# A decayed linear attention and a mixture of experts on one core: the next unit's scores issued behind the state update, and the accumulator banks divided anew

## The chip, the core and the metric

The kernel runs on one core of a Trainium2 chip. The metric is the device time of one execution in microseconds (us). The engines of the core work in parallel, each through its own queue in order: TensorE (PE in the profile, its weight loads as PEld), VectorE (DVE), ScalarE (ACT), GpSimd (POOL) and the queue SP, which issues DMAs. TensorE writes into the accumulator memory PSUM, here divided into eight banks of 512 float32 values for each of 128 partitions. VectorE and ScalarE read it from there.

## The reference

```python
batch, n_heads, seq, head_dim = (4, 8, 768, 48)          # r, k, v, w: (4, 8, 768, 48); u: (8, 48)
for t in range(S):
    cur = einsum('bhd,bhe->bhde', u * k[t], v[t])
    y[t] = einsum('bhd,bhde->bhe', r[t], state + cur)
    state = w[t][..., None] * state + einsum('bhd,bhe->bhde', k[t], v[t])
x = y.transpose(0, 2, 1, 3).reshape(3072, 384)           # tokens x (heads * head_dim)
p = domain_probs / (domain_probs.sum(-1, keepdims=True) + 1e-9)      # 3072 x 4 experts
for e in range(4):                                       # w1: 4 x 384 x 1024, w2: 4 x 1024 x 384
    out += p[:, e:e+1] * (maximum(x @ w1[e], 0) @ w2[e])
```

All arrays are float32.

## The kernel before

**Units.** The 768 steps are cut into 6 chunks of 128; a chunk of one of the 4 batches is a unit, numbered n = 4 * chunk + batch (0 to 23). A unit has these parts, each with its tile names:
- running products of the decays in both directions (`g` in `after_decays`, `e` in `until_decays`, both scans on VectorE, the second behind two short operations on `zst`), and the multiplication of r and k by them (`scale`, two VectorE operations);
- the scores of k against r, `sc`, 16 TensorE instructions (`scores`), and in the same function k turned round by four transposes into `kt`, which ScalarE copies to `ks`;
- the diagonal from r, k and u (`own_product` on GpSimd, `diag_sum`, `place`), into which `masking` puts the scores under a mask (VectorE) to give `a`;
- the sums `yp`: the state times r, and v times `a` (`values`). ScalarE and VectorE evict them as a high and a low part, and four DMAs (`fill`) put them where the experts read them, as `x`. In chunk 0 there is no state; the sums are then evicted in one copy, as plain float32;
- the new state from `ks` and v (`up`, 16 TensorE instructions), added to the old one (`carry`).

**Steps.** Units 2 to 23 go in five steps: `step_a` (next unit's `after_decays`, this unit's `scores`), `step_b` (next unit's `until_decays`), `step_c` (`masking`), `step_d` (next unit's `scale`, `diag_sum`, `place`) and `step_e` (`values`, `carry`, loads, `fill`, `guard` on ScalarE). The last chunk makes no new state, so its units have neither transposes nor update. Units 2 and 3 have an order of steps of their own; for unit 2 it is a, c, b, d, e. `go()` issues the next step.

**Experts.** A chunk of all four batches (512 tokens) goes through an expert as 8 first products (`f1`: 9 matmuls into one tile `pf1`, read by ScalarE for `hh` (L417) and then by VectorE for `hl` (L418)) and then, for each batch, a second product (`f2`: 24 matmuls into `pf2`). Between them the function `between` gives out steps at a set pace, so that the units' TensorE work lies between the experts' matmuls. Chunk 0 is done first, then chunks 1 and 2 together, then chunks 3, 4 and 5, each group with all experts in turn. From 575 us no unit is left.

**The start.** The first first products use the plain float32 sums of chunk 0, one batch at a time: `begin(b, f)` is `f1` for one batch of 128 tokens, 6 matmuls (L405), of which the start has 8 for batch 0 and 8 for batch 1. Each is a tile of its own in `pf1`, though it fills a quarter of a bank. The order around them is written out by hand (lines 583 to 653 of the file). From tile 3 of batch 0 on it reads

```python
begin(0, 3); until_decays(2); begin(0, 4); begin(0, 5); scale(2); diag_sum(2)
begin(0, 6); split_w2(1); place(2, 0); place(2, 1); begin(0, 7)
begin(1, 0); step_a(2); begin(1, 1); step_c(2); begin(1, 2); split_w2(2); guard(1)
begin(1, 3); step_b(2); begin(1, 4); step_d(2); begin(1, 5); step_e(2)
begin(1, 6); split_w2(3); begin(1, 7); step_a(3)
```

(a shortening of it, without the loads). Batches 2 and 3 follow in tiles of 256 tokens.

**Banks.** `ps_f1` has 3 banks (tiles `pf1`, and the sums of chunk 0), `ps_f2` 2, `ps_sc` one tile of 2 banks, which `sc` and `yp` use in turn, and `ps_mi` 1, which `kt`, `up` and one tile at the end use in turn.

Of the kernel before, what the change touches and what calls it, by code (L numbers as in the profile page):

```python
# [8 lines left out]
F32 = mybir.dt.float32  # L9
# [4 lines left out]
ALU = mybir.AluOpType  # L14
AX = mybir.AxisListType
PS = bass.MemoryType.PSUM

B, H, S, D = 4, 8, 768, 48
NT, DM = B * S, H * D
NE, FF = 4, 1024  # L20
C = 128
NCH = S // C
NP = H // 2
ROWS = 64 + D
KT = DM // 128
# [21 lines left out]
def chunked_path(ctx, tc, dmaj, tmaj, u_bc, probs, w1, w2, out, flag):  # L47
    nc = tc.nc

    def pool(name, bufs, space=None):  # L50
        kw = {} if space is None else {"space": space}
        return ctx.enter_context(tc.tile_pool(name=name, bufs=bufs, **kw))
# [8 lines left out]
    p_wx = pool("wx", 3)  # L61
    p_one = pool("one", 1)
    p_two = pool("two", 2)
    ps_f1 = pool("ps_f1", 3, PS)
    ps_f2 = pool("ps_f2", 2, PS)
    ps_sc = pool("ps_sc", 1, PS)
    ps_mi = pool("ps_mi", 1, PS)


    ident = const.tile([128, 128], F32, name="ident")  # L70
# [6 lines left out]
    st = [const.tile([ROWS, NP, D], F32, name=f"st{b}") for b in range(B)]  # L77
# [4 lines left out]
    sd = [const.tile([ROWS, NP * D + G], F32, name=f"sd{i}") for i in range(2)]  # L82
# [5 lines left out]
    def half(j):  # L88
        return slice(64 * j, 64 * j + D)

    def wide(j):

        return slice(64 * j, 64 if j == 0 else ROWS)
# [67 lines left out]
    un, xb, spare = {}, {}, []  # L161
    NU = B * NCH
# [103 lines left out]
    def scores(n):  # L266

        s = un[n]
        sc = ps_sc.tile([128, 2, NP, C], F32, name="sc", tag="sc")
        for i in range(NP):  # L270
            for j in range(2):
                nc.tensor.matmul(sc[:, j, i, :], s["kk"][half(j), i, :], s["rr"][half(j), i, :],  # L272
                                 start=True, stop=True)
        last = s["c"] == NCH - 1
        if not last:
            kt = ps_mi.tile([128, NP, 128], F32, name="kt", tag="mi")
            for i in range(NP):
                nc.tensor.transpose(kt[:, i, 0:ROWS], s["kk"][:, i, :], ident[0:ROWS, 0:ROWS])  # L278
        s["sc"] = sc
        if not last:  # L280
            ks = p_one.tile([128, NP, ROWS], F32, name="ks", tag="ks")
            nc.scalar.copy(ks, kt[:, :, 0:ROWS])
            s["ks"] = ks
# [6 lines left out]
    def values(n):  # L290
        s = un[n]
        c, b, v = s["c"], s["b"], s["v"]
        if c not in xb:
            xb[c] = p_x.tile([128, KT, B, 2, C], F32R, name="x", tag="x")
        x = xb[c]
        if c == 0:

            y = ps_f1.tile([128, B * C], F32, name="pf1", tag="pf1")[:, 0:KT * C].rearrange("p (i t) -> p i t", i=KT)
            z = vz[n % 2]
            for i in range(KT):  # L300
                for j in range(2):
                    nc.tensor.matmul(y[64 * j:64 * (j + 1), i, :], z[:, j, i, :], s["a"][j][:, KT, :],  # L302
                                     start=(i == 0), stop=False, skip_group_check=True)
                for j in range(2):
                    h = 2 * i + j
                    nc.tensor.matmul(y[half(j), i, :], v[:, h * D:(h + 1) * D], s["a"][j][:, i, :],  # L306
                                     start=False, stop=(i == KT - 1), skip_group_check=True)
            nc.scalar.copy(x_own()[:, :, b], y)
            return


        yp = ps_sc.tile([128, 2, NP, C], F32, name="yp", tag="sc")
        y = [yp[:, i % 2, i // 2, :] for i in range(NP)]
        for i in range(NP):
            for j in range(2):
                o = j ^ (i % 2)
                nc.tensor.matmul(y[i][wide(o)], sd[n % 2][half(j), i * D:i * D + (64 if o == 0 else D)],  # L317
                                 s["rr"][half(j), i, :], start=(i < 2), stop=False, skip_group_check=True)
        for i in range(NP):
            for j in range(2):  # L320
                h = 2 * i + j
                nc.tensor.matmul(y[i][half(j ^ (i % 2))], v[:, h * D:(h + 1) * D], s["a"][j][:, i, :],  # L322
                                 start=False, stop=(i >= 2), skip_group_check=True)
        y3 = s["y3"] = p_two.tile([ROWS, 2, 2, C], F32R, name="y3", tag="y3")

        places = (y3, yp[0:ROWS, 1, 0:2]), (x[0:ROWS, 0::2, b], yp[0:ROWS, 0, 0:2])
        for dst, src in places:
            nc.scalar.copy(dst[:, :, 0], src)  # L328
        for dst, src in places:
            nc.vector.tensor_tensor(dst[:, :, 1], src, dst[:, :, 0].bitcast(F32), ALU.subtract)  # L330

    def last_pair(n):

# [3 lines left out]
    def x_own():  # L337

        if len(spare) < 2:
            spare.append(p_acc.tile([128, B, DM], F32, name="acc", tag="acc").rearrange("p b d -> p (b d)"))  # L340
        return spare[1].rearrange("p (k b t) -> p k b t", k=KT, b=B)
# [14 lines left out]
                              in_=y3[half(1 - j), 1].bitcast(F32))  # L356
            nc.sync.dma_start(out=x[half(j), 1, s["b"]].bitcast(F32), in_=y3[half(1 - j), 0].bitcast(F32))

    def carry(n):
        s = un[n]  # L360
        c, b, v = s["c"], s["b"], s["v"]
        if c == NCH - 1:
            return
        up = ps_mi.tile([128, NP, D], F32, name="up", tag="mi")
        for i in range(NP):
            for j in range(2):
                h = 2 * i + j
                nc.tensor.matmul(up[wide(j), i, :], s["ks"][:, i, wide(j)], v[:, h * D:(h + 1) * D],  # L368
                                 start=True, stop=True)
        if c == 0:  # L370
            nc.scalar.copy(st[b], up[0:ROWS])
        else:
            nc.vector.tensor_tensor(st[b], sd[n % 2][:, 0:NP * D].rearrange("p (i e) -> p i e", i=NP), up[0:ROWS],
                                    ALU.add)

    def guard(n):

# [7 lines left out]
        return big  # L385

    def flag_it(big):
        row = ps_mi.tile([1, 128], F32, name="row", tag="mi")
        nc.tensor.transpose(row[:, 0:ROWS], big, ident[0:ROWS, 0:ROWS])
        one = p_one.tile([1, 1], F32, name="one", tag="one")  # L390
        nc.vector.tensor_reduce(one, row[:, 0:ROWS], AX.X, ALU.max)
        nc.vector.tensor_scalar(flag, one, 0.0, None, ALU.is_gt)


    ht, acc = {}, {}

    def f1(e, blk, f, t0, nt, plain):
        q, o = divmod(f, FT // NQ)
        x = xb[blk]
        fs, ts, bs = slice(o * 128, (o + 1) * 128), slice(t0, t0 + nt), slice(t0 // C, (t0 + nt) // C)  # L400
        p = ps_f1.tile([128, B * C], F32, name="pf1", tag="pf1")
        if plain:
            ww = w1_own[:, q].rearrange("p (k f) -> p k f", k=KT)
            for k in range(KT):
                nc.tensor.matmul(p[:, 0:nt], ww[:, k, fs], x_own()[:, k, bs, :],  # L405
                                 start=(k == 0), stop=(k == KT - 1))
        else:
            wh, wl = wt[e, 1, q]
            for k in range(KT):
                for n, (wv, i) in enumerate(((wh, 0), (wh, 1), (wl, 0))):  # L410
                    nc.tensor.matmul(p[:, 0:nt], wv[:, k, fs], x[:, k, bs, i, :],  # L411
                                     start=(k == 0 and n == 0), stop=(k == KT - 1 and n == 2))
        if t0 == 0:
            ht[f] = (p_h.tile([128, B * C], F32R, name="hh", tag="hh"),
                     p_h.tile([128, B * C], F32R, name="hl", tag="hl"))
        hh, hl = ht[f]
        nc.scalar.activation(hh[:, ts], p[:, 0:nt], AF.Relu)  # L417
        nc.vector.scalar_tensor_tensor(hl[:, ts], p[:, 0:nt], 0.0, hh[:, ts].bitcast(F32), ALU.max, ALU.subtract)  # L418
# [35 lines left out]
    def step_a(n):  # L454
        if n + 1 < NU:
            after_decays(n + 1)
        scores(n)
        load(n + 2, "k")
        if n + 1 < NU:
            own_product(n + 1)  # L460
# [13 lines left out]

    def step_e(n):
        values(n)
        carry(n)
        load(n + 2, "r")
        fill(n)
        if 3 < n + 1 < NU:  # L480
            guard(n + 1)
            load(n + 3, "w")
        load(n + 2, "v")
        if n == NU - 1:
            un[n]["big"] = verdict()
        elif n >= B:
            del un[n]
# [70 lines left out]
    with tc.manual_schedule():  # L558
# [24 lines left out]
        own_product(1)  # L583
        after_decays(1)
        scores(0)
        for what in ("k", "r"):
            load(2, what)
        load_own(3)
# [4 lines left out]
        until_decays(1)  # L593
        values(0)
        diag_sum(1)
        carry(0)
        load(2, "v")
        place(1, 0)
        scale(1)
# [6 lines left out]

        begin(0, 0)
        scores(1)
        for what in ("k", "r"):
            load(3, what)  # L610
        for q in range(2):
# [8 lines left out]
        load(3, "w")  # L620
        split_w2(0)
        values(1)
        carry(1)
        load(3, "v")
        begin(0, 3)
        until_decays(2)
# [27 lines left out]
        for pi, (g, e) in enumerate(passes):  # L654
            first, last = pi % NE == 0, pi % NE == NE - 1
# [221 lines left out]
```

## Time and profile before

| | |
|---|---|
| median of 3 runs | 913.03 us (912.9 to 913.32) |
| the profiled execution | 913.18 us, its span 911.5 us |
| TensorE busy | 899.6 us, 99% of the span |
| VectorE, ScalarE, GpSimd busy | 39%, 28%, 29% |
| mean granted TensorE clock | 0.998 |

The span is the time from the first to the last instruction; the profiled execution took 1.7 us beyond it. The profile names a group of instructions by line of the kernel, engine, operation and tiles (out <- in). The chain of waits is followed back from the last instruction: each piece is work that the end had to wait for. In a timeline, "[0.88 <-DVE hl L418]" says that the engine was idle for 0.88 us before the instruction, until the named one was done.

### The profile page before, as it was taken

Reading aid. Unit: us, or ns where it says so; the run is one execution under the profiler, and the core shown is the slowest. Engines: PE = TensorE matmul, PEld = TensorE weight load, DVE = VectorE, ACT = ScalarE, POOL = GpSimd, SP = SyncE. Lnnn points to the kernel's source line nnn. Section 1 sums busy time; section 2 is a strip of 40 time slices with the busy share of each in tenths; the row PEclk is TensorE's granted clock in tenths of the full one; section 3 lists DMA queues with packets and bytes.
Section 4 is the critical chain, followed back from the end, with each engine's and each line's share of the span. In section 5 each row is a group of like instructions: output and inputs, shape, how many; then the busy total and the mean of one; then the engine's idle time right before and its main releaser. Section 6 shows DMA issues by size and latency. Waiting matters only on the chain.

```text
span 911.5 us, 13796 instructions
## 1 busy us (share of the span) xinstructions
PE 899.6 (99%) x5675; PEld 810.2 (89%) x5675; DVE 351.5 (39%) x564; ACT 257.8 (28%) x482; POOL 267.1 (29%) x278
## 2 busy tenths in 40 slices
PE   8999999999999999999999999999999999999997
PEld 6898989898898988998989889899899899889987
DVE  6756555546363622122455642202222221221221
ACT  4555343322234132133221332232212310321110
POOL 3638766622255332033312220042003300230000
PEclk9999999999999999999999999999999999999999
DMA  9625435441334222111324210021002200110001
GB/s 249 196 65 180 158 119 170 137 129 56 93 105 147 67 70 68 35 58 65 105 72 131 75 49 29 1 79 61 1 1 70 69 1 1 35 35 36 18 18 38
DMA packets 36423, 70.48 MB, mean 77 GB/s; under 512 B 5376, under 2 KB 15488, under 8 KB 36352
## 3 DMA queue, kind: packets, MB, share of 16 engines
q1 hardware_dynamic: 36352, 69.53, 24.7%
q8 instruction: 46, 0.75, 0.4%
q14 instruction: 25, 0.20, 0.1%
HBM read 60.86 MB, written 4.72 MB: 72 GB/s over the span
## 4 chain that ended last, share of the span: by engine, by line
PE 98%; ACT 1%; DVE 1%; issue 0%; POOL 0%; DVEq 0%; ACTq 0%; POOLq 0%
PE pf L431 44%; PE pf L411 41%; PE sc L272 3%; PE yp L322 2%; PE pf L405 2%; PE yp L317 1%; PE kt L278 1%; PE up L368 1%; PE pf L115 1%; ACT a L227 0%; PE pf L215 0%; PE pf L302 0%; PE pf L306 0%; DVE zst L251 0%; ACT wx L380 0%; DVE a L288 0%
## 5 line engine op out<-in xcount | busy, mean ns | idle before, releaser
L411 PE MATMUL pf<-x,w1h 128*128 128x512 f32 x1104 | 342.0, 391 | 0.0
L431 PE MATMUL pf<-w2h,hh 128*128 128x384 f32 x768 | 259.7, 338 | 0.0
L431 PE MATMUL pf<-w2h,hl 128*128 128x384 f32 x768 | 257.2, 335 | 0.0
L431 PE MATMUL pf<-w2l,hh 128*128 128x384 f32 x768 | 256.9, 335 | 0.0
L418 DVE SCALAR_TENSOR_TENSOR hl<-pf,hh 128x512 fp32r<-128x512 f32 (+2 forms) x208 | 134.7, 649 | 285.0 <-ACT hh L417 284.3
L411 PEld LDWEIGHTS pf<-x,w1h 128*128 128x128 f32 x1104 | 205.8, 188 | 42.4 <-issue 0.4
L417 ACT ACTIVATE hh<-pf 128x512 fp32r<-128x512 f32 (+2 forms) x208 | 117.2, 565 | 428.1 <-PE pf L411 417.0
L411 PE MATMUL pf<-x,w1l 128*128 128x512 f32 x552 | 215.2, 390 | 0.0
L156 POOL TENSOR_TENSOR w1l<-raw,w1h 128x384 fp32r<-128x384 f32 x72 | 74.8, 1068 | 253.0 <-ACT w1h L151 253.0
L431 PEld LDWEIGHTS pf<-w2h,hh 128*128 128x128 f32 x768 | 144.2, 188 | 2.2 <-issue 0.4
L431 PEld LDWEIGHTS pf<-w2l,hh 128*128 128x128 f32 x768 | 144.2, 188 | 0.9
L431 PEld LDWEIGHTS pf<-w2h,hl 128*128 128x128 f32 x768 | 144.1, 188 | 0.0
L411 PEld LDWEIGHTS pf<-x,w1l 128*128 128x128 f32 x552 | 103.6, 188 | 21.7
L440 DVE SCALAR_TENSOR_TENSOR acc<-pf,pr,acc 128x384 f32<-128x384 f32 x72 | 44.5, 618 | 201.1 <-PE pf L431 201.1
L156 POOL TENSOR_TENSOR w2l<-raw,w2h 128x384 fp32r<-128x384 f32 x80 | 84.6, 1079 | 115.3 <-ACT w2h L151 104.5
L229 POOL TENSOR_TENSOR a<-ident,dg 128x512 f32<-128x512 f32 x42 | 44.7, 1084 | 125.9 <-DVE dg L218 121.9
L241 DVE TENSOR_TENSOR_SCAN g<-wx,ones 112x516 f32<-112x516 f32 x24 | 33.1, 1381 | 1.6 <-DMA wx<-in_dmaj 1.6
L151 ACT CAST w2h<-raw 128x768 fp32r<-128x768 f32 x40 | 33.0, 826 | 0.0
L328 ACT CAST y<-yp 112x256 fp32r<-112x256 f32 x20 | 7.5, 373 | 89.6 <-PE yp L322 88.6
L288 DVE COPY_PREDICATED a<-mask,sc 128x512 f32<-128x512 uint32 x48 | 32.2, 726 | 1.0 <-POOL a L229 0.7
L438 ACT ACTIVATE acc<-pf,pr 128x384 f32<-128x384 f32 x24 | 14.0, 581 | 64.4 <-PE pf L431 64.2
L253 DVE TENSOR_TENSOR_SCAN e<-wx,zst 112x516 f32<-112x516 f32 x24 | 31.8, 1324 | 0.8
(76 smaller groups left out, 495.1 us busy)
## 6 DMA issues: line engine op xcount, KB each, us to landing
raw<-in_w SPq DMA_DIRECT2D x76, 384.0 KB, 3.1
rkt<-in_tmaj SPq DMA_DIRECT2D x20, 384.0 KB, 3.1
wx<-in_dmaj SPq DMA_DIRECT2D x24, 226.2 KB, 3.1
k<-in_dmaj SPq DMA_DIRECT2D x24, 224.0 KB, 3.2
r<-in_dmaj SPq DMA_DIRECT2D x24, 224.0 KB, 3.4
v<-in_tmaj SPq DMA_DIRECT2D x24, 192.0 KB, 2.7
out<-acc SPq DMA_DIRECT2D x24, 192.0 KB, 1.9
x<-y SPq DMA_DIRECT2D x80, 48.0 KB, 2.2
```

Of the source, the lines that this page charges most:

```text
L151: nc.scalar.copy(hi, t)
L156: eng.tensor_tensor(lo[:, s], t[:, s], hi[:, s].bitcast(F32), ALU.subtract)
L229: nc.gpsimd.tensor_tensor(a, ident.unsqueeze(1).to_broadcast([128, NP, C]), dg[:, q].unsqueeze(2).to_broadcast([128, NP, C]), ALU.mult)
L241: nc.vector.tensor_tensor_scan(g[:, WLEN - 1:0:-1], wx[:, WLEN - 1:0:-1], ones1[:, WLEN - 1:0:-1], 0.0, ALU.mult, ALU.add)
L253: nc.vector.tensor_tensor_scan(e, wx[:, 0:WLEN - 1], zst.rearrange("p i t -> p (i t)"), 0.0, ALU.mult, ALU.add)
L272: nc.tensor.matmul(sc[:, j, i, :], s["kk"][half(j), i, :], s["rr"][half(j), i, :], start=True, stop=True)
L288: nc.vector.copy_predicated(s["a"][j], mask.unsqueeze(1).to_broadcast([128, NP, C]), s["sc"][:, j])
L411: nc.tensor.matmul(p[:, 0:nt], wv[:, k, fs], x[:, k, bs, i, :], start=(k == 0 and n == 0), stop=(k == KT - 1 and n == 2))
L417: nc.scalar.activation(hh[:, ts], p[:, 0:nt], AF.Relu)
L418: nc.vector.scalar_tensor_tensor(hl[:, ts], p[:, 0:nt], 0.0, hh[:, ts].bitcast(F32), ALU.max, ALU.subtract)
L431: nc.tensor.matmul(p, hv[:, ts], wv[:, o, :], start=(f == 0 and n == 0), stop=(f == FT - 1 and n == 2))
L440: nc.vector.scalar_tensor_tensor(a[:, b, :], p, sc, a[:, b, :], ALU.mult, ALU.add)
```

## The change

- `ps_f1` goes from 3 banks to 2. `ps_mi` goes; `ps_y` comes, one tile of 2 banks. `ps_sc` now holds scores alone. `kt`, the sums (those of chunk 0 too) and `up` lie in the tile of `ps_y` of their unit: `kt` in bank 1, the sums in both banks (chunk 0: bank 0), `up` behind the sums in bank 0 (chunk 0: bank 1).
- `scores` issues the scores alone; the transposes become `turned`, which stays in `step_a`. From unit 5 on the scores of unit n + 1 are issued in `step_e` of unit n, behind its `values`.
- `carry` is divided: its matmuls become `products`, called in `values` between the sums' matmuls and their evictions; the rest, the new state's eviction, follows the sums' evictions.
- In the start, two tiles of 128 tokens share one `pf1` bank: an even f takes a new bank, the odd f behind it the next quarter of the same one.

```diff
-    ps_f1 = pool("ps_f1", 3, PS)
+    ps_f1 = pool("ps_f1", 2, PS)
     ps_f2 = pool("ps_f2", 2, PS)
     ps_sc = pool("ps_sc", 1, PS)
-    ps_mi = pool("ps_mi", 1, PS)
+    ps_y = pool("ps_y", 1, PS)
...
+    def turned(n):
+        s = un[n]
+        y = s["y"] = ps_y.tile([128, 2, NP, C], F32, name="yp", tag="yp")
+        if s["c"] < NCH - 1:
+            kt = y[:, 1]
             for i in range(NP):
                 nc.tensor.transpose(kt[:, i, 0:ROWS], s["kk"][:, i, :], ident[0:ROWS, 0:ROWS])
             ks = p_one.tile([128, NP, ROWS], F32, name="ks", tag="ks")
             nc.scalar.copy(ks, kt[:, :, 0:ROWS])
...
-        yp = ps_sc.tile([128, 2, NP, C], F32, name="yp", tag="sc")
+        yp = s["y"]
...
+        products(n)
         y3 = s["y3"] = p_two.tile([ROWS, 2, 2, C], F32R, name="y3", tag="y3")
...
+        carry(n)
...
+    def products(n):
+        s = un[n]
+        c, v = s["c"], s["v"]
+        if c == NCH - 1:
+            return
+        o = NP * C if c == 0 else 2 * C
+        up = s["y"].rearrange("p g i t -> p (g i t)")[:, o:o + NP * D].rearrange("p (i e) -> p i e", i=NP)
         for i in range(NP):
             for j in range(2):
                 h = 2 * i + j
                 nc.tensor.matmul(up[wide(j), i, :], s["ks"][:, i, wide(j)], v[:, h * D:(h + 1) * D],
                                  start=True, stop=True)
...
-        p = ps_f1.tile([128, B * C], F32, name="pf1", tag="pf1")
+        if nt > C or f % 2 == 0:
+            narrow[:] = [ps_f1.tile([128, B * C], F32, name="pf1", tag="pf1")]
+        p = narrow[0][:, f % 2 * nt:] if nt == C else narrow[0]
...
 def step_a(n):
     if n + 1 < NU:
         after_decays(n + 1)
-    scores(n)
+    if n <= B:
+        scores(n)
+    turned(n)
...
 def step_e(n):
     values(n)
-    carry(n)
+    if B < n + 1 < NU:
+        scores(n + 1)
     load(n + 2, "r")
     fill(n)
```

More of the change, by code (lines that the diff above doesn't have):

```diff
@@ L273, in scores @@
                                  start=True, stop=True)
-        last = s["c"] == NCH - 1
-        if not last:
-            kt = ps_mi.tile([128, NP, 128], F32, name="kt", tag="mi")
+        s["sc"] = sc
+    def turned(n):
[3 more added lines that the diff above has]
+            kt = y[:, 1]
             for i in range(NP):
                 nc.tensor.transpose(kt[:, i, 0:ROWS], s["kk"][:, i, :], ident[0:ROWS, 0:ROWS])
-        s["sc"] = sc
-        if not last:
             ks = p_one.tile([128, NP, ROWS], F32, name="ks", tag="ks")
@@ L296, in values @@
         if c == 0:
-            y = ps_f1.tile([128, B * C], F32, name="pf1", tag="pf1")[:, 0:KT * C].rearrange("p (i t) -> p i t", i=KT)
+            y = s["y"][:, 0, 0:KT]
             z = vz[n % 2]
@@ L323, in values @@
                                  start=False, stop=(i >= 2), skip_group_check=True)
+        products(n)
         y3 = s["y3"] = p_two.tile([ROWS, 2, 2, C], F32R, name="y3", tag="y3")
@@ L330, in values @@
             nc.vector.tensor_tensor(dst[:, :, 1], src, dst[:, :, 0].bitcast(F32), ALU.subtract)
+        carry(n)
     def last_pair(n):
@@ L357, in fill @@
             nc.sync.dma_start(out=x[half(j), 1, s["b"]].bitcast(F32), in_=y3[half(1 - j), 0].bitcast(F32))
-    def carry(n):
+    def products(n):
         s = un[n]
-        c, b, v = s["c"], s["b"], s["v"]
+        c, v = s["c"], s["v"]
         if c == NCH - 1:
             return
-        up = ps_mi.tile([128, NP, D], F32, name="up", tag="mi")
+        o = NP * C if c == 0 else 2 * C
+        up = s["y"].rearrange("p g i t -> p (g i t)")[:, o:o + NP * D].rearrange("p (i e) -> p i e", i=NP)
+        s["up"] = up
         for i in range(NP):
@@ L369, in carry @@
                                  start=True, stop=True)
+    def carry(n):
+        s = un[n]
+        c, b = s["c"], s["b"]
+        if c == NCH - 1:
+            return
         if c == 0:
-            nc.scalar.copy(st[b], up[0:ROWS])
+            nc.scalar.copy(st[b], s["up"][0:ROWS])
         else:
-            nc.vector.tensor_tensor(st[b], sd[n % 2][:, 0:NP * D].rearrange("p (i e) -> p i e", i=NP), up[0:ROWS],
-                                    ALU.add)
+            nc.vector.tensor_tensor(st[b], sd[n % 2][:, 0:NP * D].rearrange("p (i e) -> p i e", i=NP),
+                                    s["up"][0:ROWS], ALU.add)
     def guard(n):
@@ L387, in flag_it @@
     def flag_it(big):
-        row = ps_mi.tile([1, 128], F32, name="row", tag="mi")
+        row = ps_y.tile([128, 2, NP, C], F32, name="yp", tag="yp")[0:1, 0, 0]
         nc.tensor.transpose(row[:, 0:ROWS], big, ident[0:ROWS, 0:ROWS])
@@ L392, in flag_it @@
         nc.vector.tensor_scalar(flag, one, 0.0, None, ALU.is_gt)
-    ht, acc = {}, {}
+    ht, acc, narrow = {}, {}, []
     def f1(e, blk, f, t0, nt, plain):
@@ L585, in chunked_path @@
         scores(0)
+        turned(0)
         for what in ("k", "r"):
@@ L595, in chunked_path @@
         diag_sum(1)
-        carry(0)
         load(2, "v")
@@ L608, in chunked_path @@
         scores(1)
+        turned(1)
         for what in ("k", "r"):
@@ L622, in chunked_path @@
         values(1)
-        carry(1)
         load(3, "v")
```

## The prediction

> **What bounds the kernel now.** I read the page first: its span, the engines' busy time, and the chain of waits by engine.
>
> ```profile
> span 911.5 us, 13796 instructions
> ...
> PE 899.6 (99%) x5675; PEld 810.2 (89%) x5675; DVE 351.5 (39%) x564; ACT 257.8 (28%) x482; POOL 267.1 (29%) x278
> ...
> PE 98%; ACT 1%; DVE 1%; issue 0%; POOL 0%; DVEq 0%; ACTq 0%; POOLq 0%
> ```
>
> TensorE is busy for 899.6 of 911.5 us and is 98% of the chain. So two things can move the time: TensorE's own work with the changes between its kinds of matmul, and new waits of TensorE, each of which lengthens the run by its full length, since nothing later can make it good. The other engines count only where TensorE waits for them. Then I read the chain in order of time, where one unit's work, undisturbed expert work, and units of the last chunk can be set side by side (start, duration, what):
>
> ```profile
> 95.62 0.45 PE up L368 x14
> 96.07 2.31 PE pf L431 x12
> 98.38 1.09 PE sc L272 x16
> 99.47 0.53 PE kt L278 x4
> 100.00 10.45 PE pf L431 x60
> ...
> 333.42 16.66 PE pf L431 x96
> 350.08 16.36 PE pf L411 x72
> ...
> 518.93 8.53 PE pf L431 x48
> 527.46 0.60 PE yp L317 x12
> 528.05 1.01 PE yp L322 x16
> 529.06 2.28 PE pf L431 x12
> ```
>
> Undisturbed, a second-product matmul costs 16.66 / 96 = 0.1735 us, a first-product tile of nine 16.36 / 8 = 2.045 us. What lies above that in a piece is the price of coming back from a unit's work: 2.31 - 12 x 0.1735 = 0.23 us behind the update, 10.45 - 60 x 0.1735 = 0.04 behind the transposes, 8.53 - 48 x 0.1735 = 0.20 behind scores alone (the piece at 518.93 follows scores of the last chunk), 2.28 - 2.08 = 0.20 behind sums alone.
>
> **Part 1: scores moved behind the update, units 5 to 23.** No instruction is saved; what changes is which kinds are neighbours on TensorE. Before, a unit of chunks 1 to 4 costs 1.09 + 0.53 + 0.04 in step a and 0.60 + 1.01 + 0.45 + 0.23 in step e, 3.95 us. After: 0.53 + 0.04, and 0.60 + 1.01 + 0.45 + 1.09 + 0.20, 3.92 us, a saving of 0.03. Not in the rows are the change from update to scores, which comes new, and the change from scores to transposes, which goes; a return costs 0.04 to 0.23 in the rows, so each lies between 0 and 0.2, and the saving of a unit between -0.15 and 0.25. I take 0.10, since coming back from transposes, at 0.04, is the cheap kind, and the transposes now stand alone between experts' matmuls. That is 15 units (5 to 19) x 0.10 = 1.5 us. The units of the last chunk have no transposes, so their step a goes altogether: of 1.09 + 0.20 the 0.20 goes, and 4 units (20 to 23) x 0.20 = 0.8 us. Together -2.3 us, with ends at +1.4 and -4.6.
>
> Behind the moved scores stand the expert matmuls in TensorE's queue, so they must not wait. They need r and k scaled by VectorE in step d, one step earlier. One place is tight, unit 5 behind unit 4's update (two rows of the timeline):
>
> ```profile
> 71.43 0.68 DVE L264 TENSOR_TENSOR k<-k,g 112x512 f32<-112x512 f32 x1
> ...
> 71.56 0.44 PE L431 MATMUL pf<-w2h,hh 128*128 128x384 f32 x1
> ```
>
> The scaling ends at 72.11 and the place of the scores is 71.56, so the wait is 0 to 0.6 us; I take 0.3, because VectorE may have caught up by then. SP's queue keeps its order; the load of the next r behind the scores can be issued up to 1.09 us later, and its data are wanted a whole unit later (16 us or more in the chain).
>
> **Part 2: the update ahead of the evictions.** The same 16 instructions at the same place on TensorE. The sums' evictions on ScalarE and VectorE, and the four DMAs of `fill` behind them, come up to the update's 0.45 us later. They feed chunks that the experts read later, and the bank they free is wanted by the transposes of the next unit, at least one piece of 2.31 us later. I cost it at 0; without this cover it would be 0.45 us a unit.
>
> **Part 3: two banks for the first products.** A tile now waits for the reads of the last tile but one, not of the one before that. Rows by shape and two places in the timeline:
>
> ```profile
> L418 DVE SCALAR_TENSOR_TENSOR hl<-pf,hh 128x512 fp32r<-128x512 f32 x184 | 127.1, 691 | 269.8 <-ACT hh L417 269.1
> ...
> L417 ACT ACTIVATE hh<-pf 128x512 fp32r<-128x512 f32 x184 | 110.1, 599 | 417.2 <-PE pf L411 417.0
> ```
>
> ```profile
> 83.58 0.62 PE L411 MATMUL pf<-x,w1h 128*128 128x512 f32 x2
> 83.64 1.47 DVE L418 SCALAR_TENSOR_TENSOR hl<-pf,hh 128x512 fp32r<-128x512 f32 x2
> ...
> 126.04 0.66 DVE L418 SCALAR_TENSOR_TENSOR hl<-pf,hh 128x512 fp32r<-128x512 f32 x1
> ...
> 126.49 0.62 PE L411 MATMUL pf<-x,w1h 128*128 128x512 f32 x2
> ```
>
> The two reads take 599 + 691 ns, 1.3 us, against 2.045 us for the tile in between, so with nothing in front of them they are hidden, and from 575 us on nothing is. Where a unit's VectorE work comes first, they are late. At 83.64 two second reads follow each other; the first ends about 84.3, and the tile that will need its bank starts at 83.58, so 0.7 us. At 126.04 the read ends at 126.70 against 126.49, so 0.2 us. I found no other in the stretches with units: +0.9 us, with ends at 0 (the shifted steps miss these places) and 3 (they hit others).
>
> **Part 4: two narrow tiles in one bank, the start.** This decides. First VectorE's timeline and then TensorE's, from 24 to 40 us:
>
> ```profile
> 24.80 1.23 DVE L253 TENSOR_TENSOR_SCAN e<-wx,zst 112x516 f32<-112x516 f32 x1
> 25.95 0.46 DVE L418 SCALAR_TENSOR_TENSOR hl<-pf,hh 128x128 fp32r<-128x128 f32 x2
> 26.33 0.68 DVE L263 TENSOR_TENSOR r<-r,e 112x512 f32<-112x512 f32 x1
> 26.93 0.69 DVE L264 TENSOR_TENSOR k<-k,g 112x512 f32<-112x512 f32 x1
> ...
> 31.76 1.35 DVE L288 COPY_PREDICATED a<-mask,sc 128x512 f32<-128x512 uint32 x2 [0.69 <-POOL a L229]
> 33.01 0.27 DVE L418 SCALAR_TENSOR_TENSOR hl<-pf,hh 128x128 fp32r<-128x128 f32 x1
> ...
> 33.96 1.95 DVE L251 TENSOR_SCALAR zst<-g 112x4 f32<-112x4 f32 x1
> 35.94 0.18 DVE L252 RECIPROCAL zst<-zst 112x4 f32<-112x4 f32 x1
> 36.16 1.23 DVE L253 TENSOR_TENSOR_SCAN e<-wx,zst 112x516 f32<-112x516 f32 x1
> 37.31 0.27 DVE L418 SCALAR_TENSOR_TENSOR hl<-pf,hh 128x128 fp32r<-128x128 f32 x1
> ```
>
> ```profile
> 25.01 0.95 PE L215 MATMUL pf<-u_col,acc 112*128 112x2 f32 x8
> ...
> 28.00 1.16 PE L272 MATMUL sc<-r,k 48*128 48x128 f32 x16
> ...
> 33.02 1.05 PE L215 MATMUL pf<-u_col,acc 112*128 112x2 f32 x8 [0.62 <-POOL acc L192]
> ...
> 37.63 1.60 PE L405 MATMUL pf<-acc,x 128*128 128x128 f32 x12 [0.88 <-DVE hl L418]
> 39.17 1.05 PE L272 MATMUL sc<-r,k 48*128 48x128 f32 x14
> ```
>
> The trace has no matmul that writes beside data being read from the same bank. The nearest row is the one at 37.63: a tile that takes over a bank starts 0.05 us after the last read of that bank ends (37.31 + 0.27). I take it that an odd tile, too, waits until VectorE has read the even tile beside it; the other end is that it waits for nothing. A narrow tile takes (39.17 - 37.63) / 2 = 0.77 us, so an odd tile right behind its even one is at TensorE long before the reads, and what VectorE has in its queue ahead of the second read is now on TensorE's path (the waits below are estimates from these rows):
> - Batch 0, tile 5 (in its place at 25.01 - 0.77 = 24.2): tile 4's read stands behind the scan and ends at about 26.2 (half of the row at 25.95). Wait 1.9 us.
> - Tile 7: the read of tile 6 stands behind that of tile 5, now late, and both scalings (0.68 + 0.69). Wait 0.8 us. The scores at 28.00 move to 30.7.
> - Batch 1, tile 1: step a's matmuls lie between; no wait. Tile 3: the read of tile 2 stands behind `masking` (1.35), which starts with the read of tile 1 done, about 0.75 after tile 1. So it ends 0.75 + 1.35 + 0.27 = 2.4 us after tile 1, where tile 3 could start 0.77 after it. Wait 1.7 us.
> - Tile 5: the read of tile 4 stands behind step b. Tile 3's reads end 0.9 us after the tile, then come `zst` (0.2 without a neighbour, 1.95 in this row), 0.18, 1.23 and the read of 0.27, so 2.8 us after tile 3; TensorE has tile 4 and the small L215 group, 1.6 us. Wait 1.2 us, 3 with the long `zst`; I take 1.5.
> - Tile 7: the sums' and the state's copies on ScalarE now start behind the update, and the first read of tile 6 comes after both; the second ends about 1.5 us after the tile's start. Wait 0.7 us.
>
> That is 6.6 us. Before, TensorE idles in the same stretch for 0.62 and 0.88 us, waits that fall inside these (the second because sums of chunk 0 took a `pf1` bank, which is no longer so). The scores at 39.17 therefore come 5.1 us later, with ends at -0.9 (no wait in the bank, the 0.88 gone) and +7. Behind them the chain is TensorE alone, so the end moves by as much.
>
> [...]
>
> **The sum.** 913.18 - 2.3 + 0.3 + 0.9 + 5.1 = 917.2 us for the profiled execution, which stands 0.15 above the median of the runs shown; against that median 917.0 us.
>
> **The rivals.**
> - *The pair shares a bank without waiting.* Place: the odd tiles between 24 and 44 us. Then the start gains the 0.88 and the sum is 913.0 - 2.3 + 0.3 + 0.9 - 0.9 = 911.0 us, faster. It decides if the start's new waits come to less than about 1 us. For it: a quarter of a bank each, no shared data. Against it: the row at 37.63, and that VectorE and ScalarE are then reading the bank. Chance 0.10.
> - *The start's waits mostly overlap waits that were there.* TensorE idles 1.5 us there now, and GpSimd, which the row at 31.76 waits for, may set the pace of both kernels. With 2 to 2.5 us left of 5.1 the time is 914.2 us. For it: several engines take turns in that chain. Against it: each wait above is behind VectorE work that is issued after the earlier wait, so they add. Chance 0.18.
> - *The two-bank ring also binds in the plain stretches.* 0.745 us of slack (2.045 - 1.3) less the latencies between; if 0.1 us were missing at each of 60 tiles with nothing around them, 923 us. Against it: nothing in those stretches delays the reads. Chance 0.04.
> - *The waits of the start and -2.3 + 0.3 + 0.9 as forecast*: chance 0.68, its own range 915 to 919.5.
>
> **How the numbers follow.** About 0.2% (1.8 us) is what can be told from no change: below 911.2 faster, above 914.9 slower. Faster: most of the first rival and a little of the second with part 1 at its good end, 0.11. Same: the rest of the first, the greater part of the second, and a small part of the forecast, 0.19. Slower: 0.70. The range 912.0 to 920.0 leaves out most of the first and all of the third rival, and the long `zst`.
>
> **What would show it.** In the changed profile: the first scores of unit 3 at about 44 us, not 39.17, with idle time on L405 put down to VectorE's L418 (right), or none (the first rival). The chain should show update then scores without expert work between, and pieces of transposes alone. L411 should have 1 us of idle time released by L418, not tens. The prediction is wrong if the return behind the merged step costs much more than 0.20 us, or if VectorE's order in the start differs from the order of the code.

## The result, and the profile after

The changed kernel takes 919.97 us (median; 917.83 to 921.5), against 913.17 us (912.9 to 914.49) for the kernel before in the same comparison, four runs each: a ratio of 1.0070, 95% interval 1.0057 to 1.0082. The profiled execution is the lowest of the four, 917.83 us. The lines of after are f1 L428 (the narrow tiles L422), `hh` L434, `hl` L435, f2 L448, transposes L283, update L377.

The page of after first: span, busy time, chain by engine.

```profile
span 916.1 us, 13817 instructions
...
PE 899.1 (98%) x5675; PEld 812.5 (89%) x5675; DVE 350.3 (38%) x564; ACT 257.3 (28%) x482; POOL 265.3 (29%) x278
...
PE 96%; DVE 1%; ACT 1%; issue 1%; DMA 1%; POOL 0%; SPq 0%; DVEq 0%; POOLq 0%; ACTq 0%
```

TensorE still does the same 5675 matmuls in nearly the same busy time (899.1 us, 899.6 before), in a span 4.6 us longer: by these rows TensorE's idle time goes from 11.9 to 17.0 us. (Run 3 shows a further part that busy time hides.) Next, the waits, as total us, how often, and the longest:

```profile
PEld pf L422 <- DVE hl L435: 6.4, 5, 2.0
...
PE pf L422 <- DVE hl L435: 5.6, 5, 1.8
```

Five waits of narrow tiles for VectorE's `hl`. The timeline of TensorE in the start of after shows where they are and how far they carry:

```profile
25.91 0.94 PE L422 MATMUL pf<-acc,x 128*128 128x128 f32 x6 [1.76 <-DVE hl L435]
...
29.10 1.60 PE L422 MATMUL pf<-acc,x 128*128 128x128 f32 x12 [0.69 <-DVE hl L435]
...
35.13 1.60 PE L422 MATMUL pf<-acc,x 128*128 128x128 f32 x12 [1.44 <-DVE hl L435]
...
38.50 0.94 PE L422 MATMUL pf<-acc,x 128*128 128x128 f32 x6 [0.98 <-DVE hl L435]
...
44.48 0.94 PE L422 MATMUL pf<-acc,x 128*128 128x128 f32 x6 [0.69 <-DVE hl L435]
45.35 1.16 PE L272 MATMUL sc<-r,k 48*128 48x128 f32 x16
```

The last row is the scores of unit 3, which stood at 39.17 before: 6.2 us later. What VectorE did meanwhile, in the timeline of VectorE:

```profile
24.44 1.23 DVE L253 TENSOR_TENSOR_SCAN e<-wx,zst 112x516 f32<-112x516 f32 x1
25.59 0.27 DVE L435 SCALAR_TENSOR_TENSOR hl<-pf,hh 128x128 fp32r<-128x128 f32 x1
...
28.00 0.68 DVE L264 TENSOR_TENSOR k<-k,g 112x512 f32<-112x512 f32 x1
28.76 0.29 DVE L435 SCALAR_TENSOR_TENSOR hl<-pf,hh 128x128 fp32r<-128x128 f32 x1
...
33.57 1.33 DVE L291 COPY_PREDICATED a<-mask,sc 128x512 f32<-128x512 uint32 x2
34.80 0.28 DVE L435 SCALAR_TENSOR_TENSOR hl<-pf,hh 128x128 fp32r<-128x128 f32 x1
...
37.03 1.23 DVE L253 TENSOR_TENSOR_SCAN e<-wx,zst 112x516 f32<-112x516 f32 x1
38.18 0.27 DVE L435 SCALAR_TENSOR_TENSOR hl<-pf,hh 128x128 fp32r<-128x128 f32 x1
...
44.14 0.29 DVE L435 SCALAR_TENSOR_TENSOR hl<-pf,hh 128x128 fp32r<-128x128 f32 x1 [3.56 <-ACT hh L434]
```

At the first, third and fourth wait the read of the even tile stands behind a unit's long VectorE instruction: the scan, then `hl` until 25.86, then the odd tile at 25.91; `masking`, then `hl` until 35.08, then the odd tile at 35.13; the scan again, `hl` until 38.45, the odd tile at 38.50. At the second and the fifth nothing of VectorE's delays the read. Before the second, the even tile ends at 28.41 (27.50 + 0.91), the scaling at 28.68, and ScalarE's read only at 28.73 (28.45 + 0.28 in its timeline). VectorE's read follows from 28.76 to 29.05, and the odd tile starts at 29.10. At the fifth, VectorE has been idle for 3.56 us until `hh` is done. So 0.69 us is what an odd tile waits for the two reads alone when nothing covers them. By these rows (an estimate) four waits have this 0.69 in them, 2.8 us, and the other 2.8 are VectorE's queue: 1.76 - 0.69, 1.44 - 0.69, and the whole 0.98 of the fourth, where the L215 group of TensorE lasts 0.95 us, longer than the two reads.

Behind the start the change gains a little back. The chain of after, in order of time, for one unit of the middle and one of the last chunk (with `up` in the sums' tile, the update stands there as `yp` L377), and the piece behind the last unit:

```profile
101.09 0.60 PE yp L322 x12
101.69 1.01 PE yp L327 x16
102.70 0.44 PE yp L377 x14
103.15 1.09 PE sc L272 x16
104.24 2.30 PE pf L448 x12
106.54 0.39 PE yp L283 x4
106.92 10.42 PE pf L448 x60
...
517.04 0.60 PE yp L322 x12
517.64 1.01 PE yp L327 x16
518.65 1.09 PE sc L272 x16
519.74 2.28 PE pf L428 x9
...
579.39 0.10 PE yp L404
579.49 16.38 PE pf L428 x72
```

Sums, update and scores now follow each other without a break, and the transposes stand alone. The row at 579.39 is the small transposition behind the last unit; the chain of before has it so:

```profile
574.80 0.10 PE row L389
574.90 16.38 PE pf L411 x72
```

It comes 4.59 us later, after a start that is 6.18 us later, so 1.59 us are gained between the two. From there to the end both kernels take 336.7 us. So the loss is made before 46 us, and nothing behind 580 us matters.

### The profile page after: what moved, and what is told of

Read it like the earlier page. It is cut to its first block, busy times and chain, and to the rows that moved or that the text cites. A ratio compares the mean times of both kernels' runs of the same rounds, so it can differ in the third digit from the quotient of the medians.

```text
span 916.1 us, 13817 instructions
## 1 busy us (share of the span) xinstructions
PE 899.1 (98%) x5675; PEld 812.5 (89%) x5675; DVE 350.3 (38%) x564; ACT 257.3 (28%) x482; POOL 265.3 (29%) x278
## 4 chain that ended last, share of the span: by engine, by line
PE 96%; DVE 1%; ACT 1%; issue 1%; DMA 1%; POOL 0%; SPq 0%; DVEq 0%; POOLq 0%; ACTq 0%
PE pf L448 44%; PE pf L428 41%; PE sc L272 3%; PE pf L422 2%; PE yp L327 2%; PE yp L322 1%; PE yp L377 1%; PE yp L283 1%; DMA r<-in_dmaj 1%; DVE e L253 0%; PE yp L305 0%; PE yp L309 0%; DVE hl L435 0%; ACT hh L434 0%; PE pf L215 0%
## 5 line engine op out<-in xcount | busy, mean ns | idle before, releaser
L428 PE MATMUL pf<-x,w1h 128*128 128x512 f32 x1104 | 342.2, 391 | 0.1
L448 PE MATMUL pf<-w2h,hh 128*128 128x384 f32 x768 | 259.5, 338 | 0.0
L448 PE MATMUL pf<-w2h,hl 128*128 128x384 f32 x768 | 257.1, 335 | 0.0
L448 PE MATMUL pf<-w2l,hh 128*128 128x384 f32 x768 | 256.7, 334 | 0.0
L435 DVE SCALAR_TENSOR_TENSOR hl<-pf,hh 128x512 fp32r<-128x512 f32 (+2 forms) x208 | 134.9, 649 | 288.6 <-ACT hh L434 288.1
L428 PEld LDWEIGHTS pf<-x,w1h 128*128 128x128 f32 x1104 | 205.7, 188 | 43.4 <-DVE hl L435 1.3
L434 ACT ACTIVATE hh<-pf 128x512 fp32r<-128x512 f32 (+2 forms) x208 | 117.5, 565 | 433.2 <-PE pf L428 420.0
L428 PE MATMUL pf<-x,w1l 128*128 128x512 f32 x552 | 215.3, 390 | 0.0
L448 PEld LDWEIGHTS pf<-w2h,hh 128*128 128x128 f32 x768 | 144.2, 188 | 2.7 <-issue 0.2
L156 POOL TENSOR_TENSOR w1l<-raw,w1h 128x384 fp32r<-128x384 f32 x72 | 72.4, 1035 | 252.4 <-ACT w1h L151 250.9
L448 PEld LDWEIGHTS pf<-w2l,hh 128*128 128x128 f32 x768 | 144.2, 188 | 0.9
L448 PEld LDWEIGHTS pf<-w2h,hl 128*128 128x128 f32 x768 | 144.2, 188 | 0.0
L428 PEld LDWEIGHTS pf<-x,w1l 128*128 128x128 f32 x552 | 103.6, 188 | 21.9
```

What stands on the lines that cost most here:

```text
L156: eng.tensor_tensor(lo[:, s], t[:, s], hi[:, s].bitcast(F32), ALU.subtract)
L448: nc.tensor.matmul(p, hv[:, ts], wv[:, o, :], start=(f == 0 and n == 0), stop=(f == FT - 1 and n == 2))
```

## The experiments

All times are medians against the kernel before on the same chip. In the first set, `own_tile`, `share_only`, `filler` and `four_banks`, it took 913.35 us (20 runs); in the second set, the other four, 913.13 us (24 runs). Each set ran on a chip of its own, so runs 5, 6 and 8, which start from run 4, are compared with it across the two chips.

**1. A bank for each narrow tile again**, the rest of the change as it is, with two banks:

```diff
-        if nt > C or f % 2 == 0:
-            narrow[:] = [ps_f1.tile([128, B * C], F32, name="pf1", tag="pf1")]
-        p = narrow[0][:, f % 2 * nt:] if nt == C else narrow[0]
+        p = ps_f1.tile([128, B * C], F32, name="pf1", tag="pf1")
```

> The changed kernel, but every narrow first-product tile of the start takes a bank of its own again, out of the two that are left. Theory (the odd tile of a pair waits until the even one has been read): those five waits, 5.6 us of idle time before L422 in the changed profile, go; what is left is the ring of two, by the trace of before 1 to 2.5 us in the start. The scores of unit 3 come at 40 to 42 us instead of 45.35, the granted clock stays at 1.0 from 36 to 46 us, and the time is 912.5 to 914.5 us. Rival (two banks instead of three are the cost, and sharing is not): 917 us or more, scores of unit 3 at 44 us or later.

Measured: 913.42 us (911.88 to 914.24, 11 runs), ratio 0.9991 (0.9982 to 1.0000). Its waits:

```profile
PEld pf L420 <- DVE hl L433: 2.2, 5, 1.2
...
PE pf L420 <- DVE hl L433: 1.0, 1, 1.0
```

One wait of 1.0 us for TensorE is left of five with 5.6. With nothing but the pair undone, the loss is gone.

**2. The pair alone**, in the kernel before: three banks, the old order, and only the three lines of the pair added.

> The kernel before, with three banks and its old order of steps, and only the pairs of narrow tiles in one bank taken from the change. Theory: the odd tiles wait here as well; the scores of unit 3 come at 43 to 45.5 us instead of 39.17, the clock may fall to a half for one stretch of some 3.4 us, and the time is 917 to 921 us. Rival (sharing costs nothing as long as there are three banks): 913 us, as before.

Measured: 919.37 us (917.95 to 921.14, 6 runs), ratio 1.0063 (1.0049 to 1.0077). In its waits stands the same row as in after:

```profile
PE pf L407 <- DVE hl L420: 5.6, 5, 1.8
```

So the pair alone makes the five waits and a loss as large as that of the whole change, with three banks too; the count of banks and the order behind it are not needed for it. Part of these 6.2 us between the profiled executions (919.37 and 913.18) is a stretch of half clock of 3.41 us (last section). It begins at 21.38 us, ahead of the first wait of a narrow tile (27.66 us in this run), so those waits did not bring it on; the lowest runs of both kernels lie 5.2 us apart.

**3. The same waits, filled with work.** After, with matmuls of zeros into an idle `pf2` tile just ahead of the five waiting tiles; this adds work that the reference does not have.

```diff
+IDLE = {(0, 5): 9, (0, 7): 3, (1, 3): 7, (1, 5): 5, (1, 7): 3}
...
+        if nt == C and (t0 // C, f) in IDLE:
+            d = ps_f2.tile([128, DM], F32, name="pf2", tag="pf2")
+            for _ in range(IDLE[t0 // C, f]):
+                nc.tensor.matmul(d, zero[:, 0:128], zero[:, 0:DM], start=True, stop=True)
```

> The changed kernel, and in front of the five odd tiles that wait, 9, 3, 7, 5 and 3 matmuls of zeros into a bank that nobody reads, a little less work than each wait. The waits stay. Theory (idle TensorE time in the start makes the clock fall, and that is 1.6 us of the profiled run and most of the scatter of 917.8 to 921.5 us): granted clock 1.0 throughout, scores of unit 3 at 43.3 to 44.5 us, time 915.5 to 916.8 us with all runs within 0.6 us. Rival (the clock falls for another reason): half clock near 40 us remains, 918 to 921 us with the same scatter.

Measured: 916.12 us (915.98 to 918.18, 6 runs), ratio 1.0034 (1.0022 to 1.0046). The median was as expected; that all runs would lie together was a miss, since two of the six are 2 us above the others. What it tells is in the profile. The table by windows of after (the columns are length; busy us of TensorE, its weight loads, VectorE, ScalarE and GpSimd, with counts; granted clock; DMA share; GB/s):

```profile
39.00:40.00 1.00, 1.00 (x16) 0.88 (x17) 1.00 (x2) 0.31 (x2) 0.82 (x2) 1.00 0.88 321
40.00:41.00 1.00, 1.00 (x16) 1.00 (x13) 0.58 (x2) 0.00 (x0) 0.00 (x0) 0.52 0.08 31
...
43.00:44.00 1.00, 0.79 (x5) 0.60 (x4) 0.00 (x0) 0.33 (x2) 0.00 (x0) 0.77 0.46 104
```

and of the one with the waits filled:

```profile
40.00:41.00 1.00, 1.00 (x29) 1.00 (x26) 0.59 (x2) 0.00 (x0) 0.00 (x0) 1.00 0.06 21
```

The clock of after is at half speed from 40.0 to 43.4 us, and 16 matmuls fit where 29 did. Up to there the two executions agree to 0.01 us, as the tile behind the fourth wait shows in TensorE's timeline of the filled kernel, 38.51 against 38.50 in after:

```profile
38.51 0.94 PE L427 MATMUL pf<-acc,x 128*128 128x128 f32 x6
...
43.77 1.16 PE L273 MATMUL sc<-r,k 48*128 48x128 f32 x16
```

Its scores of unit 3 come at 43.77, in after at 45.35. So of the 6.18 us of the start 1.58 are the half clock, and 4.6 are the waits with what comes with them: the five of after less the two of before are 5.56 - 1.50 = 4.1, and the other 0.5 is not divided further here. The profiled executions' times, 916.1 against 917.83, have the same difference of 1.6 to 1.7. That the waits brought the half clock on is likely in this execution, since it goes when they are filled, but it rests on one profile of each.

**4. No sharing, four banks for the narrow tiles.** The banks of `pf2` lie idle in the start; the odd tiles go there.

```diff
+        if nt == C and f % 2:
+            p = ps_f2.tile([128, DM], F32, name="pf2", tag="pf2")
+        else:
+            p = ps_f1.tile([128, B * C], F32, name="pf1", tag="pf1")
```

> The changed kernel, but the odd narrow tiles of the start take tiles of ps_f2, which has no second product to hold yet, so that four banks turn. Theory: almost no wait of TensorE on L435 in the start, scores of unit 3 at 38.5 to 40 us, clock 1.0; from there the change's gain of 3.2 us by merged steps and its 1.7 us of new waits (unit 5's scores 0.7, the ring of two 1.0) remain: 911 to 912.5 us, faster than before. Rival (the moved scores cost as much as they gain): 913 to 914 us.

Measured: 911.10 us (910.58 to 912.97, 7 runs), ratio 0.9978 (0.9967 to 0.9989): below both kernels. No narrow tile waits for `hl` any more; TensorE's timeline in the same stretch has only these waits:

```profile
32.44 1.05 PE L215 MATMUL pf<-u_col,acc 112*128 112x2 f32 x8 [0.63 <-POOL acc L192]
33.75 0.94 PE L423 MATMUL pf<-acc,x 128*128 128x128 f32 x6 [0.26 <-ACT dg L216]
...
38.25 1.16 PE L272 MATMUL sc<-r,k 48*128 48x128 f32 x16
```

The scores of unit 3 are 0.9 us earlier than before the change, and 1.6 more are gained behind them as in after: 913.18 - 0.9 - 1.6 = 910.7, and the profiled execution took 910.58. Runs 5, 6 and 8 start from this kernel, since nothing of the pair is left in its start.

**5. Scores back in step a**, all else as in 4 (`scores(n)` always in `step_a`, none in `step_e`).

> As four_banks, but the scores stand in step a again, ahead of the transposes, for all units. Theory (the merged step saves 0.16 us in units 5 to 19 and 0.2 in 20 to 23, 3.2 us in all, and costs 0.7 us where unit 5's scores wait for VectorE): 2.3 to 2.9 us more than four_banks, 913.2 to 914 us, and no wait of unit 5's scores. Rival (the gain of four_banks over the kernel before comes from the sums leaving the banks of the first products, not from the scores): within 0.7 us of four_banks, 910.8 to 911.8 us.

Measured: 915.04 us (913.7 to 916.86, 11 runs), ratio 1.0020 (1.0011 to 1.0030). The profiled execution is 913.70, 3.1 us over that of 4, a little more than expected; the medians are 3.9 apart, and the median of 915.04 lies outside the range expected. The move of the scores is a gain of some 3 us, net of the wait of unit 5's scores, and without it the two-bank kernel would be behind the kernel before even with four banks in the start.

**6. The update behind the evictions**, all else as in 4 (`products(n)` moved behind the copies and subtractions of the sums).

> As four_banks, but the update's matmuls come behind the evictions of the sums, still in the bank that holds half of these sums. Theory (TensorE waits until the last read from a bank is done before it writes beside the data): each of the 16 units of chunks 1 to 4 waits for both copies on ScalarE and both subtractions on VectorE, 1.4 to 2 us, so 933 to 943 us. The figure of the prediction for this cover, 0.45 us a unit, would give 918 to 920 us. Rival (no wait beside the data): 911 us.

Measured: 952.38 us (945.32 to 957.06, 4 runs), ratio 1.0442 (1.0416 to 1.0469), above the range expected. Its waits, first that of the weight loads, then that of the matmuls themselves:

```profile
PEld yp L377 <- DVE x L335: 29.6, 16, 2.3
PE yp L377 <- DVE x L335: 25.5, 16, 2.1
...
PE yp L377 <- ACT acc L311: 2.3, 4, 0.6
```

Sixteen updates, those of chunks 1 to 4, wait for the last subtraction of the sums, 1.6 us each (1.85 by the weight loads), and the four of chunk 0 for the copy of theirs. Those 27.8 us of the matmuls, of 34.7 between the profiled executions (945.32 and 910.58), are most of the difference; two stretches of half clock lie in it as well, and the sizes of the other parts are not separated here. The update of chunk 0 writes the other bank of the same tile than the one that is read, and waits all the same. So what the program waits for is not shown to be the bank: it may be the tile. The same holds for the pair of the start, which is one tile too. Whether two separate tiles within one bank would wait was not tried.

**7. Two banks alone**, in the kernel before (`pool("ps_f1", 2, PS)`).

> The kernel before with two banks in place of three for the first products and nothing else changed; one bank lies idle. Theory (ring of two): one late read each near 79.5 and 122 us, 0.9 us together, and in the start waits for the reads of the last tile but one, with the sums of chunk 0 in the same ring, 2 to 4 us; 915.5 to 918.5 us, with half clock in some runs. Rival (three banks are not needed): 913 to 914 us.

Measured: 916.47 us (915.92 to 917.6, 8 runs), ratio 1.0033 (1.0022 to 1.0044), as expected.

```profile
PEld pf L405 <- DVE hl L418: 2.2, 5, 1.2
PEld pf L411 <- DVE hl L418: 1.5, 2, 1.0
...
PE pf L302 <- DVE hl L418: 0.8, 1, 0.8
```

The loss of a bank costs waits in the start (L405, and the sums of chunk 0, L302) and behind units (L411), and none at the 60 tiles of the plain stretches, where 72 matmuls take 16.36 us as before.

**8. To take away what is left of the scatter**: 4, with the scores moved from unit 6 on only, and eight matmuls of zeros in a gap of TensorE at 18 us (added work).

> As four_banks, with the scores moved from unit 6 on instead of unit 5, and 8 matmuls of zeros ahead of unit 1's sums, where TensorE is idle for 1.65 us in all kernels here. Theory: unit 5's wait of 0.7 us goes for 0.16 of saving, and the clock stays at 1.0 in the first 40 us, so that the runs lie within 0.7 us of each other: 910.0 to 910.8 us. Rival (the clock falls in some runs for another reason): median as four_banks, with runs of 912 us and more among them.

Measured: 912.14 us (910.53 to 913.73, 11 runs), ratio 0.9986 (0.9977 to 0.9995): a miss. The lowest runs are those of 4, 910.5 to 911.0, but the others still lie 1 to 3 us above. What makes these steps in a kernel whose profiled start is at full clock (1.00 in every window of 3 us up to 42 us) stays open.

## Why the prediction was right

Forecast 917.0 us, measured 919.97 in the median and 917.83 in the profiled execution, the one that the terms are checked against. The mechanism that decides was right: the odd tiles wait, and their waits outweigh the rest. A term was missing, one was too small, and two of the five waits had another reason than the one given. That the median too lies within 912.0 to 920.0, by 0.03 us, is luck: the sum has no term for what lifts the other three runs.

- *Part 4, the pair.* The five waits were forecast, in order, at 1.9, 0.8, 1.7, 1.5 and 0.7 us, and measured 1.76, 0.69, 1.44, 0.98 and 0.69. The first, third and fourth came behind the VectorE instructions named. The second was put down to VectorE's scalings and the fifth to ScalarE's copies; both were the bare time of the two reads. The scaling ended before `hh` did (28.68 against 28.73), and the copies had ended at 43.15, 0.7 us before `hh` began. That their sizes came out near is luck. The net of part 4 was forecast at +5.1 and is +4.6. This rules out the first rival (the pair does not wait) and the second (the waits overlap old ones, with 2 to 2.5 us left). Run 2 shows that they need nothing else of the change. The premise, that an odd tile waits for the read of the even one, was taken from one row of before, the tile at 37.63, and the trace of after bears it out: five waits, 5.6 us, each ended 0.05 us after that read (25.91 behind 25.86, 44.48 behind 44.43).
- *The scores of unit 3*, forecast at about 44, came at 45.35. With the waits alone they come at 43.77, as run 3 shows. The rest is the term that the sum did not have: half clock for 3.4 us, +1.6. The step that failed is the bound of part 4: it counted the waits by their length and had nothing for the clock.
- *Part 1.* Forecast -2.3. By the rows of after a unit of the middle costs 0.60 + 1.01 + 0.44 + 1.09 + (2.30 - 2.08) + 0.39 + 0.01 = 3.76 us, against 3.95 by the rows of before: 0.19 a unit, 2.85 for 15 units. The last chunk saves 0.17 a unit, 0.7 for 4. So -3.5 by rows. What the stretch leaves gives -3.2: it gained 1.59 in all, with 0.6 and 1.0 lost in it to the two items that follow. Run 5 shows 3.1 net of unit 5's wait, so some -3.7 if nothing else differs. Within the ends given (+1.4 to -4.6); 0.10 a unit was too little, because the transposes by themselves cost 0.39 with almost no return, not 0.53, and update to scores needs no change that shows.
- *Unit 5's scores* were forecast to wait 0.3 (0 to 0.6). The waits on `k` of after, in its timeline of TensorE:

```profile
78.44 1.16 PE L272 MATMUL sc<-r,k 48*128 48x128 f32 x16 [0.62 <-DVE k L264]
```

- *Part 3, the ring of two.* Forecast +0.9 at two places; in the waits of after

```profile
PEld pf L428 <- DVE hl L435: 1.3, 3, 0.5
```

three places, at 90.5, 133.5 and 176.3 us in the timeline of the weight loads. The stretches of 72, 72 and 63 first-product matmuls around them lose 0.4, 0.4 and 0.2 us against 2.045 a tile, +1.0 (an estimate from the chain). Two are the tiles named, the fifth and the sixth of their stretches, forecast at 0.7 and 0.2; the third was missed. None lies in the plain stretches, which rules out the third rival.
- *Part 2, the update ahead of the evictions*, cost nothing, as forecast: ahead of none of the 80 transposes (L283) does TensorE wait in after. Its 0.45 us a unit is the price if the later evictions were not covered; no run tests that. Run 6 has the other order, the update behind the evictions. There a unit pays 1.6 us at the matmuls, because the update then waits for the reads of the sums, and not the update's own length.

The sum with the measured terms: 913.18 + 4.6 + 1.6 - 3.2 + 0.6 + 1.0 = 917.8 us, against 917.83. It has to close, because -3.2 was taken from what was left; with -3.5 by rows it is 917.5. The other three runs of after lie 1.7, 2.6 and 3.7 us higher, and their mean granted clocks are 0.995, 0.993 and 0.993 instead of 0.997. A loss of 0.004 of 918 us is 3.7 us, so more time at half clock would account for them. That is not shown: in which part of those runs the clock fell is not recorded.

## What to carry to other kernels

Before two small tiles share one, count for the second write the reads of the first (0.69 us here when nothing covers them), and on top of that what the reader's queue holds ahead of these reads (up to 1.07 us here). Count an idle stretch of TensorE by its length, and keep a margin for the clock: a stretch of half clock took 1.58 us of after (run 3), and what brings one on is open. When a bank must be saved, save it where its reader is idle: here the banks of the second products stood empty in the start, and using them turned a loss of 0.7% into a gain of 0.2%.

## What the hardware showed that was not expected

The clock. Ahead of the last few microseconds, the kept profiles have five stretches of half clock: one in after, one each in runs 1 and 2, two in run 6. Each is one of 3.41 us at 0.50. The mean granted clock of the profiled executions is 0.997 in the three with one stretch, 0.996 in run 6 and 0.998 or 0.999 in the others. Run 3 puts the cost of one at 1.58 us; by its length it would be 3.41 / 2 = 1.7 at full use, an estimate. The windows of that length in after, the last at half clock (length; busy TensorE with its count; clock; DMA share; GB/s):

```profile
22.98:26.39 3.41, 1.65 (x15) 1.00 0.75 245
...
36.62:40.03 3.41, 2.43 (x27) 1.00 0.77 249
40.03:43.44 3.41, 3.41 (x37) 0.50 0.03 8
```

and the same in the kernel with the pair alone:

```profile
17.97:21.38 3.41, 1.55 (x18) 1.00 1.02 322
21.38:24.79 3.41, 3.41 (x38) 0.50 0.58 196
```

Ahead of the drop TensorE was busy for 2.43 us of 3.41 (71%) in after and 1.55 (45%) in the pair alone, never idle throughout. But the window of after with 1.65 us was not followed by a drop, so the share of one window alone does not decide it; what does is open. The stretch of run 1, at 11.6 to 15.0 us, and that of the pair alone, from 21.38 us, lie ahead of any wait of a narrow tile, so the waits of the pair are not their only cause.
